# The second layer's output products as seven sums of half the tokens (Strassen), in a kernel whose in-products already go that way

## Chip, cores, metric

One core of a Trainium2 chip. The metric is the device time of one launch in microseconds; below is the median of three runs. All data start and end in device memory.

## What is computed

The reference is a linear-attention block (decayed scores in blocks of 64, a running state) followed by two feed-forward layers in float32. Only the layers matter here; tokens are 1536, of which the first 512 are a block of their own and the other 1024 (two blocks of 512) are "the token pair":

```python
x = x @ w_in                     # 1536 x 512 by 512 x 2048
x = np.maximum(x, 0.0) ** 2
x = x @ w_out                    # layer 1, back to 512
gate = 1.0 / (1.0 + np.exp(-(x @ w_gate)))   # layer 2, 512 x 1536
val = x @ w_val
out = gate * val @ w_out         # 1536 x 1536 by 1536 x 512
```

## The kernel before

Float32 products are made of reduced-precision float32 (`F32R`): each operand is split into a high part (a cast, on ScalarE) and a low part (what the cast lost, a subtraction on VectorE), and three products high x high, high x low, low x high are added up in PSUM. So every 128 x 128 tile of weights costs three matmuls for a block of 512 tokens.

Program order is written out by hand. A list of dated jobs (`at(pos, job)`) hangs on a clock that counts the planned TensorE time (`passed(us)`); a job is put into the engines' queues when the clock passes its date. The date only places the job among its neighbours in each queue: an engine takes its queue strictly in order and runs ahead as far as data and free buffers allow. Loads and stores go through SyncE's queue (SP).

Order of work: attention; layer 1 for the first 512 tokens (`step_1`); layer 1's in-products for the token pair by Strassen (`strassen`, one key is one 256 x 256 product in seven blocks of six matmuls); its output products (`pair_out(1)`); then the same for layer 2: `step_2`, `strassen` with twelve keys (gate and val in turn), `pair_out(2)`. T5 is the planned moment at which the last of these begins.

In a key, block A11 is snapped by ScalarE (`snap`, giving `s1`), then come S1 (`s5`), S2 (`s2`), S4, S3, A12 and A22. VectorE makes the sums (`total`, L559). A gate sum goes through a sigmoid on ScalarE (L651), a val sum is multiplied with the gate on VectorE (L655) and stored to device memory (`g_dram`). Blocks S1 and S4 share a bank, A11, S2, S3 and A22 another: the next block on a bank starts only when its reader is done.

`pair_out(2)` walks the twelve rows f of 128 hidden units. For each, `load_out` fetches the stored product (128 x 1024) and the output weights (128 x 512), `split_out` splits both, and 24 matmuls of 512 columns add to eight banks (four rows of output, two blocks of tokens). With the last f, each bank is copied and sent out as it ends.

Of the kernel before, what the change touches and what calls it, by code (L numbers as in the profile page):

```python
# [34 lines left out]
MM = 0.2267  # L35
# [5 lines left out]
def retention_moe_kernel(  # L41
# [24 lines left out]
    nc = tc.nc  # L66
# [5 lines left out]
    NF2 = w2.shape[0]  # L72
# [5 lines left out]
    wp = ctx.enter_context(tc.tile_pool(name="wp", bufs=27))  # L78
# [16 lines left out]
    def at(pos, fn):  # L95
        agenda.append((pos, len(agenda), fn))
# [7 lines left out]
    def passed(us):  # L104
        clock[0] += us
        flush()
# [140 lines left out]
    xr = {}  # L247
# [190 lines left out]
    def evacuate(ph):  # L438
# [17 lines left out]
    a_t, as_t, s_t = {}, {}, {}  # L456
    g_dram = {
        1: dram.tile([NF1, P, 2, TB], F32, name="g1"),
        2: dram.tile([NF2, P, 2, TB], F32, name="g2"),
    }  # L460
    A11, A12, A22 = (0, 0), (0, 1), (0, 3)
    S3, S4, S1, S2 = (1, 0), (1, 1), (1, 2), (1, 3)
# [155 lines left out]
        held.clear()  # L618

    held = []  # L620

    def keep_g(ph, f, t, g):
        held.append(lambda: nc.sync.dma_start(out=g_dram[ph][f, :, t], in_=g))

    def pair_in_1(i):
        def use(di, t, c, in_psum):
# [51 lines left out]
    def prepare_out(ph, f, pos):  # L678
        at(pos - 16.0, lambda: load_out(ph, f))
        at(pos - 6.5, lambda: split_out(f))  # L680

    def pair_out(ph):
        nf = NF1 if ph == 1 else NF2
        acc = {}
        for f in range(nf):
            (wh, wl), (gh, gl) = wos_t.pop(f), gs_t.pop(f)
            first, last = f == 0, f == nf - 1
            order = [(e, t) for t in range(2) for e in range(4)]
            if last:
                order = [(e, t) for e in range(4) for t in range(2)]  # L690
            for e, t in order:
                if first:
                    acc[e, t] = bank()
                for i, (a, b) in enumerate(((wh, gh), (wh, gl), (wl, gh))):
                    nc.tensor.matmul(  # L695
                        acc[e, t], lhsT=a[:, e * P : (e + 1) * P], rhs=b[:, t, :],
                        start=first and i == 0, stop=last and i == 2,
                    )
                passed(3 * MM)
                if last:  # L700
                    copy = nc.scalar.copy if t == 0 else nc.vector.tensor_copy
                    if ph == 1:
                        copy(xr[t + 1][:, e, :], acc[e, t])
                        continue
                    o = unit("o")
                    dst = out[e, :, (t + 1) * TB : (t + 2) * TB]
                    if (e, t) != (3, 1):
                        copy(o, acc[e, t])
                        (nc.scalar if t == 0 else nc.sync).dma_start(out=dst, in_=o)
                        continue  # L710
                    a, b = slice(0, TB // 2), slice(TB // 2, TB)
                    nc.scalar.copy(o[:, a], acc[e, t][:, a])
                    nc.vector.tensor_copy(o[:, b], acc[e, t][:, b])
                    nc.scalar.dma_start(out=dst[:, a], in_=o[:, a])
                    nc.sync.dma_start(out=dst[:, b], in_=o[:, b])


    order = ORDER
    lead = LEAD
# [18 lines left out]
    for k in range(lead, NCH):  # L738
        a, b = SLOTS[k - lead]
# [196 lines left out]
```

## Time and profile before

| | |
|---|---|
| median of three runs | 603.05 us (602.11 to 603.96) |
| span of the profiled execution, first to last instruction | 599.4 us; no time of its own is listed for it, and 3.65 us lie between it and the median |
| TensorE matmuls busy | 582.6 us, 97% of the span |
| TensorE weight loads busy (beside matmuls) | 478.8 us, 80% |
| VectorE busy | 448.6 us, 75% |
| ScalarE busy | 332.5 us, 55% |
| output products, both layers (L695) | 672 matmuls of 512 columns |

A matmul's recorded length (390 ns) is longer than its distance to the next, since matmuls overlap; the distance from start to start is what counts. An engine's idle time matters only where TensorE waits for it.

### The profile page before, as it was taken

The numbers are of one execution on the slowest core, as the hardware profiler recorded it, in microseconds if no ns is written. First come the engines' busy times: TensorE is split into PE (matmuls) and PEld (weight loads), VectorE is DVE, ScalarE is ACT, GpSimd is POOL, SyncE is SP. The second block draws the span as 40 slices with busy tenths as digits, with TensorE's granted clock in tenths as the row PEclk, the third lists the DMA queues.
The fourth block names the chain that finished last, engine by engine and source line by source line (L and its number), as shares of the span: only waits on it lengthen the run. The fifth ranks groups of instructions, "written<-read, shape, count | busy, mean of one in ns | idle before, by whom it ended". The sixth has DMA issues, their size and how long they took to land.

```text
span 599.4 us, 8496 instructions
## 1 busy us (share of the span) xinstructions
PE 582.6 (97%) x3076; PEld 478.8 (80%) x3076; DVE 448.6 (75%) x673; ACT 332.5 (55%) x525; POOL 36.9 (6%) x34
## 2 busy tenths in 40 slices
PE   7799999999899999999999999999999999999997
PEld 7677878887678888888888888888888888888885
DVE  0699998999888868988877788694778787569101
ACT  0367787988556456756557654554464455537101
POOL 1672212100000000000000000000000000000000
PEclk9899999999999999999999999999999999999999
DMA  7996898682145377999978945511332422658003
GB/s 212 402 418 232 306 309 331 237 297 87 57 121 208 107 240 271 408 414 415 410 276 279 312 170 172 163 50 54 122 106 106 140 81 80 209 187 357 0 1 141
DMA packets 53578, 127.19 MB, mean 212 GB/s; under 512 B 5784, under 2 KB 7584, under 8 KB 53536
## 3 DMA queue, kind: packets, MB, share of 16 engines
q1 hardware_dynamic: 52376, 124.41, 57.9%
q10 hardware_dynamic: 1160, 2.24, 1.1%
q8 instruction: 24, 0.39, 0.3%
q14 instruction: 18, 0.15, 0.1%
HBM read 90.96 MB, written 35.66 MB: 211 GB/s over the span
## 4 chain that ended last, share of the span: by engine, by line
PE 87%; DVE 4%; DMA 2%; POOL 2%; issue 2%; ACT 1%; SPq 0%; ACTq 0%; POOLq 0%; DVEq 0%
PE p L545 30%; PE p L695 25%; PE p L386 17%; PE p L400 12%; DMA kv<-in_kv 1%; POOL kd L278 1%; PE p L329 1%; PE p L322 1%; POOL qd L285 1%; DMA lam_sb<-in_lam 1%; PE p L264 1%; DVE wlo L374 1%; DVE al L526 1%; DVE m L175 1%; ACT ah L520 1%
## 5 line engine op out<-in xcount | busy, mean ns | idle before, releaser
L545 PE MATMUL p<-xcl,ah 128*128 128x512 f32 x280 | 109.1, 390 | 2.5 <-DVE xcl L469 2.5
L545 PE MATMUL p<-xch,ah 128*128 128x512 f32 x280 | 109.4, 391 | 0.4 <-ACT s L554 0.2
L545 PE MATMUL p<-xch,al 128*128 128x512 f32 x280 | 109.0, 389 | 0.0
L695 PE MATMUL p<-g2h,whi 128*128 128x512 f32 x224 | 87.1, 389 | 0.0
L695 PE MATMUL p<-g2l,whi 128*128 128x512 f32 x224 | 87.1, 389 | 0.0
L695 PE MATMUL p<-g2h,wlo 128*128 128x512 f32 x224 | 87.1, 389 | 0.0
L545 PEld LDWEIGHTS p<-xcl,ah 128*128 128x128 f32 x280 | 52.6, 188 | 13.5 <-DVE xcl L469 2.9
L545 PEld LDWEIGHTS p<-xch,ah 128*128 128x128 f32 x280 | 52.5, 188 | 12.9 <-ACT s L554 1.4
L545 PEld LDWEIGHTS p<-xch,al 128*128 128x128 f32 x280 | 52.6, 188 | 11.0
L559 DVE TENSOR_TENSOR c<-p,s 128x512 f32<-128x512 f32 x60 | 41.2, 688 | 25.3 <-PE p L545 21.4
L554 ACT COPY s<-p 128x512 f32<-128x512 f32 x60 | 35.0, 586 | 37.4 <-PE p L545 37.4
L167 DVE CUSTOM_DVE_ANT_0 u<-m,r 128x1024 uint16<-128x1024 uint16 x68 | 49.5, 728 | 2.7
L374 DVE TENSOR_TENSOR wlo<-u,whi 128x512 fp32r<-128x512 f32 x68 | 46.1, 707 | 7.0 <-ACT whi L372 5.7
L150 ACT ACTIVATE j<-raw 128x512 f32<-128x512 f32 x68 | 45.6, 671 | 10.2 <-issue 5.3
L175 DVE SCALAR_TENSOR_TENSOR m<-j,m 128x512 int32<-128x512 int32 x68 | 49.5, 728 | 1.2
L151 ACT ACTIVATE r<-raw 128x512 int32<-128x512 uint32 x68 | 45.2, 665 | 8.7 <-PE p L695 5.5
L695 PEld LDWEIGHTS p<-g2l,whi 128*128 128x128 f32 x224 | 42.0, 188 | 8.8
L695 PEld LDWEIGHTS p<-g2h,whi 128*128 128x128 f32 x224 | 42.0, 188 | 8.7
L695 PEld LDWEIGHTS p<-g2h,wlo 128*128 128x128 f32 x224 | 42.0, 188 | 8.7
L372 ACT CAST whi<-u 128x512 fp32r<-128x512 f32 x68 | 39.0, 616 | 13.7 <-DVE u L167 13.2
L386 PE MATMUL p<-xh,wlo 128*128 128x512 f32 x160 | 43.2, 392 | 1.1 <-DVE wlo L374 1.1
L386 PE MATMUL p<-xh,whi 128*128 128x512 f32 x160 | 43.8, 395 | 0.0
(87 smaller groups left out, 911.6 us busy)
## 6 DMA issues: line engine op xcount, KB each, us to landing
raw<-in_w SPq DMA_DIRECT2D x68, 512.0 KB, 7.1
w<-u SPq DMA_DIRECT2D x68, 256.0 KB, 4.0
u<-w SPq DMA_DIRECT2D x64, 256.0 KB, 5.5
g<-g SPq DMA_DIRECT2D x56, 256.0 KB, 4.4
g<-g SPq DMA_DIRECT2D x28, 512.0 KB, 7.5
a<-w SPq DMA_DIRECT2D x20, 512.0 KB, 4.3
kv<-in_kv SPq DMA_DIRECT2D x12, 512.0 KB, 8.6
qk<-in_qk SPq DMA_DIRECT2D x10, 512.0 KB, 5.7
```

Source lines behind the costliest of these rows:

```text
L150: nc.scalar.activation(j, t[:, :, 1].bitcast(F32), AF.Copy, scale=2.0**-112)
L151: nc.scalar.activation(r, t[:, :, 0].bitcast(mybir.dt.uint32), AF.Copy, scale=2.0**-29)
L167: nc.vector.tensor_tensor(out=w.bitcast(I32), in0=m, in1=r, op=ALU.add)
L175: lambda: nc.vector.scalar_tensor_tensor(out=m, in0=j, scalar=-(2**31), in1=m, op0=ALU.bitwise_and, op1=ALU.bitwise_or),
L372: nc.scalar.copy(hi, src)
L374: lambda lo=lo, src=src, hi=hi: nc.vector.tensor_tensor(out=lo, in0=src, in1=hi, op=ALU.subtract)
L386: nc.tensor.matmul(acc, lhsT=a[:, kk * P : (kk + 1) * P], rhs=b[:, kk, :], start=i == 0, stop=i == 11,)
L400: nc.tensor.matmul(acc[e], lhsT=a[:, e * P : (e + 1) * P], rhs=b, start=first and i == 0, stop=last and i == 2,)
L545: nc.tensor.matmul(acc, lhsT=w[:, col, kk * P : (kk + 1) * P], rhs=x[:, kk, :], start=start and i == 0, stop=stop and i == 5, skip_group_c ...
L554: nc.scalar.copy(s, acc)
L559: nc.vector.tensor_tensor(out=c, in0=acc, in1=s, op=ALU.add)
L695: nc.tensor.matmul(acc[e, t], lhsT=a[:, e * P : (e + 1) * P], rhs=b[:, t, :], start=first and i == 0, stop=last and i == 2,)
```

## The change

Layer 2's output products for the token pair are made by Strassen as well, over pairs i of hidden rows, halves e of the 512 outputs and the two blocks of tokens. `pair_out(2)` is replaced by `blocks_out`. The tokens of each block are cut into two halves h of 256, worked one after the other; for each h seven sums of 128 x 512 (two row tiles p of 256 columns) are kept in seven banks over all six i, and combined after the last i on VectorE into the four output blocks. Each i needs seven combinations of weights (`set_w`, once, kept for both halves) and seven of stored products (`set_g`, once for each h), each split into high and low. Weight sets 0 and 1 are made during the Strassen part before, set 2 at its end, sets 3 to 5 during the first half. Stored products lie in pairs now, so that one load brings the four quarters that a set needs. The pool `wp` has 28 buffers for 27.

```diff
+    HB = TB // 2
+    MH = 0.1152
...
+    def set_w(i, pos, lead):
...
+        def combine():
+            w0, w1 = (w.rearrange("p (e c) -> p e c", e=2) for w in wq_t[i])
+            s = quad(4, "ws", F32)
...
+            tt(out=s[:, 0], in0=w0[:, 1], in1=w0[:, 0], op=ALU.subtract)
+            tt(out=s[:, 2], in0=w0[:, 1], in1=w1[:, 1], op=ALU.add)
+            tt(out=s[:, 3], in0=w1[:, 1], in1=s[:, 0], op=ALU.add)
+            tt(out=s[:, 1], in0=w1[:, 0], in1=s[:, 3], op=ALU.subtract)
...
+            nc.scalar.copy(r[:, 0], w0[:, 0])
+            nc.scalar.copy(r[:, 1:3], w1)
+            nc.scalar.copy(c, s)
...
+            tt(out=rl[:, 0], in0=w0[:, 0], in1=rh[:, 0], op=ALU.subtract)
+            tt(out=rl[:, 1:3], in0=w1, in1=rh[:, 1:3], op=ALU.subtract)
+            tt(out=cl, in0=s, in1=ch, op=ALU.subtract)
+
+        at(pos - lead, load)
+        at(pos - 7.5, combine)
+        at(pos - 5.5, high)
+        at(pos - 3.4, low)
+
+    def set_g(h, i, pos):
...
+            tt(out=t[:, 0:2], in0=g[:, 0:1].to_broadcast([P, 2, HB]), in1=g[:, 1:4:2], op=ALU.subtract)
+            tt(out=t[:, 2], in0=g[:, 3], in1=t[:, 0], op=ALU.subtract)
+            tt(out=t[:, 3], in0=g[:, 2], in1=t[:, 2], op=ALU.subtract)
...
+            nc.scalar.copy(r, g[:, 1:4])
+            nc.scalar.copy(c, t)
...
+            nc.vector.tensor_tensor(out=rl, in0=g[:, 1:4], in1=rh, op=ALU.subtract)
+            nc.vector.tensor_tensor(out=cl, in0=t, in1=ch, op=ALU.subtract)
+
+        at(pos - 14.0, load)
+        at(pos - 7.0, combine)
+        at(pos - 5.4, high)
+        at(pos - 3.2, low)
+
+    def blocks_out():
...
+                for k, ((wp_, wc), (gp_, gc)) in where.items():
+                    if i == 0:
+                        acc[k] = bank()
+                    for p in range(2):
+                        for n, (a, b) in enumerate(((0, 0), (0, 1), (1, 0))):
+                            nc.tensor.matmul(
+                                acc[k][:, p * HB : (p + 1) * HB],
+                                lhsT=ws[a][wp_][:, wc, p * P : (p + 1) * P],
+                                rhs=gs[b][gp_][:, gc],
...
+                        passed(3 * MH)
+                        if last and h == 1 and k == 4:
+                            add("c21", 4, "u3", slice(p * HB, (p + 1) * HB))
+                            put(v["c21"], 1, 0, p)
...
+                    if k == 1:
+                        v["s1"] = unit("s1")
+                        nc.scalar.copy(v["s1"], acc[1])
+                    elif k == 2:
+                        add("c11", 2, "s1")
...
-        for f in range(NF2):
-            prepare_out(2, f, T5 + 24 * MM * f)
+        step = 42 * MH
+        for i in range(NF2 // 2):
+            pos = (T4 + 45.0, T4 + 75.0, T5 - 1.0)[i] if i < 3 else T5 + step * i - 1.5
+            set_w(i, pos, 14.0)
+            for h in range(2):
+                n = h * NF2 // 2 + i
+                set_g(h, i, T5 + step * n - (1.0 if n else 0.0))
...
-        pair_out(2)
+        blocks_out()
```

The sums are worked in the order 1, 2, 6, 5, 7, 3, 4; sums 1, 2 and 3 read the stored products as they are (`gqr`), the others their combinations (`gqt`). In the changed kernel lines behind 618 move by two or more (L655 becomes L657).

Three places show what moves in the queues. First VectorE's queue around the last key of the Strassen part, before: `c<-p,s` are the key's sums, `g<-c,r` the products with the gate, `wlo` and `g2l` low halves for the output part. The second `c<-p,s` is the one that block A22 waits for.

```order
L675 TENSOR_TENSOR wlo<-u,whi 128x512
L676 TENSOR_TENSOR g2l<-g_5222,g2h 128x1024
L559 TENSOR_TENSOR c<-p,s 128x512
L655 TENSOR_TENSOR g<-c,r 128x512
L559 TENSOR_TENSOR c<-p,s 128x512
L655 TENSOR_TENSOR g<-c,r 128x512
L559 TENSOR_TENSOR c<-p,s 128x512
L655 TENSOR_TENSOR g<-c,r 128x512
```

The same place on VectorE now, with the low halves of weight set 2 (`wqs`) and of token set 0 (`gqr`, `gqt`) and the combining of token set 1 (`gt`):

```order
L726 TENSOR_TENSOR wqs<-ws,wqs 128x1024
L559 TENSOR_TENSOR c<-p,s 128x512
L657 TENSOR_TENSOR g<-c,r 128x512
L757 TENSOR_TENSOR gqr<-gq,gqr 128x768
L758 TENSOR_TENSOR gqt<-gt,gqt 128x1024
L743 TENSOR_TENSOR gt<-gq 128x512
L744 TENSOR_TENSOR gt<-gq,gt 128x256
L745 TENSOR_TENSOR gt<-gq,gt 128x256
L559 TENSOR_TENSOR c<-p,s 128x512
L657 TENSOR_TENSOR g<-c,r 128x512
L559 TENSOR_TENSOR c<-p,s 128x512
```

Five operations stand between the first and the second sum where one stood.

Second, ScalarE's queue where a val key follows a gate key in the Strassen part, before: sigmoids `r`, high halves `ah`, copies `s` of the key's banks, of which the last two are `s5` and `s2`.

```order
L651 ACTIVATE r<-c 128x512 x3
L520 CAST ah<-a 128x1024
L554 COPY s<-p 128x512
L651 ACTIVATE r<-p 128x512
L520 CAST ah<-as 128x1024
L554 COPY s<-p 128x512 x2
```

Now, at the key that holds weight set 1 (`wq`, `ws`):

```order
L653 ACTIVATE r<-c 128x512 x3
L520 CAST ah<-a 128x1024
L554 COPY s<-p 128x512
L716 CAST wq<-wq 128x256
L717 CAST wq<-wq 128x512
L718 CAST wq<-ws 128x1024
L653 ACTIVATE r<-p 128x512
L520 CAST ah<-as 128x1024
L554 COPY s<-p 128x512 x2
```

Three casts stand between the first copy and the sigmoid ahead of the last two.

Third, VectorE's queue for one i of the first half, where before there were two operations for each f (`wlo` and `g2l`, as in the first piece); here i = 3, and i = 4 and 5 read alike:

```order
L702 TENSOR_TENSOR ws<-wq 128x256
L703 TENSOR_TENSOR ws<-wq 128x256
L704 TENSOR_TENSOR ws<-wq,ws 128x256
L705 TENSOR_TENSOR ws<-wq,ws 128x256
L743 TENSOR_TENSOR gt<-gq 128x512
L744 TENSOR_TENSOR gt<-gq,gt 128x256
L745 TENSOR_TENSOR gt<-gq,gt 128x256
L724 TENSOR_TENSOR wqr<-wq,wqr 128x256
L725 TENSOR_TENSOR wqr<-wq,wqr 128x512
L726 TENSOR_TENSOR wqs<-ws,wqs 128x1024
L757 TENSOR_TENSOR gqr<-gq,gqr 128x768
L758 TENSOR_TENSOR gqt<-gt,gqt 128x1024
```

Two f make one i, so four operations have become twelve.

## Rows read from the trace of the kernel before

**Rows 1.** The page: span, and TensorE's granted clock in 40 slices.

```profile
span 599.4 us, 8496 instructions
...
PEclk9899999999999999999999999999999999999999
```

**Rows 2.** Stretches: length, then busy time of PE, PEld, DVE, ACT, POOL, clock, DMA.

```profile
505.00:515.00 10.00, 10.00 (x45) 8.27 (x45) 8.53 (x14) 4.13 (x6) 0.00 (x0) 1.00 0.60 156
...
540.00:550.00 10.00, 10.00 (x46) 8.29 (x45) 9.48 (x11) 8.38 (x11) 0.00 (x0) 1.00 1.03 412
...
560.00:570.00 10.00, 10.00 (x46) 8.29 (x45) 0.00 (x0) 0.00 (x0) 0.00 (x0) 1.00 0.00 0
```

**Rows 3.** The chain that ended last: start, length, engine, line, count.

```profile
417.94 111.78 PE p L545 x492
529.72 64.61 PE p L695 x285
```

**Rows 4.** Timeline of TensorE: sixteen 128-column products at two clocks.

```profile
13.43 1.87 PE L264 MATMUL p<-qk 64*128 64x128 f32 x16 [0.23 <-DMA qk<-in_qk]
...
118.31 1.16 PE L264 MATMUL p<-qk 64*128 64x128 f32 x16
```

**Rows 5.** Groups of the page: weight loads of the output products (busy, mean ns, idle).

```profile
L695 PEld LDWEIGHTS p<-g2l,whi 128*128 128x128 f32 x224 | 42.0, 188 | 8.8
```

**Rows 6.** Timeline of VectorE, one key: start, length, operation.

```profile
506.45 0.69 DVE L559 TENSOR_TENSOR c<-p,s 128x512 f32<-128x512 f32 x1 [1.36 <-PE p L545]
507.18 0.69 DVE L655 TENSOR_TENSOR g<-c,r 128x512 f32<-128x512 f32 x1
507.78 0.68 DVE L559 TENSOR_TENSOR c<-p,s 128x512 f32<-128x512 f32 x1
...
511.04 0.42 DVE L513 TENSOR_TENSOR as<-a 128x256 f32<-128x256 f32 x1
511.38 0.41 DVE L514 TENSOR_TENSOR as<-as 128x256 f32<-128x256 f32 x1
...
512.65 1.21 DVE L526 TENSOR_TENSOR al<-a,ah 128x1024 fp32r<-128x1024 f32 x1
513.78 1.21 DVE L526 TENSOR_TENSOR al<-as,ah 128x1024 fp32r<-128x1024 f32 x1
```

**Rows 7.** Timeline of ScalarE in the key before the last two.

```profile
500.31 0.63 ACT L651 ACTIVATE r<-c 128x512 f32<-128x512 f32 x1 [0.73 <-DVE c L559]
500.84 1.03 ACT L520 CAST ah<-a 128x1024 fp32r<-128x1024 f32 x1
501.78 0.58 ACT L554 COPY s<-p 128x512 f32<-128x512 f32 x1
...
503.73 0.59 ACT L554 COPY s<-p 128x512 f32<-128x512 f32 x1
```

**Rows 8.** Timeline, last key: the sum, and block A22's first matmul.

```profile
527.31 0.68 DVE L559 TENSOR_TENSOR c<-p,s 128x512 f32<-128x512 f32 x1
...
528.20 0.39 PE L545 MATMUL p<-xch,ah 128*128 128x512 f32 x1
```

**Rows 9.** Timeline of TensorE: its longest wait in a Strassen part.

```profile
158.32 0.50 PE L545 MATMUL p<-xcl,ah 128*128 128x512 f32 x1 [2.52 <-DVE xcl L469]
```

**Rows 10.** A stretch behind the last product, columns as in rows 2.

```profile
597.00:597.50 0.50, 0.00 (x0) 0.00 (x0) 0.00 (x0) 0.00 (x0) 0.00 (x0) 0.87 0.82 285
```

**Rows 11.** Timeline of the end, all engines.

```profile
592.57 0.39 PE L695 MATMUL p<-g2h,wlo 128*128 128x512 f32 x1
...
593.00 0.59 ACT L708 COPY o<-p 128x512 f32<-128x512 f32 x1 [0.77 <-PE p L695]
...
594.61 0.39 PE L695 MATMUL p<-g2h,wlo 128*128 128x512 f32 x1
...
595.81 0.42 DVE L713 COPY o<-p 128x256 f32<-128x256 f32 x1 [1.44 <-ACT o L712]
596.26 0.33 SPq L715 DMA_DIRECT2D out_t<-o  x1
```

More of the change, by code (lines that the diff above doesn't have):

```diff
@@ L680, in prepare_out, with quad, load, high @@
         at(pos - 6.5, lambda: split_out(f))
+    HB = TB // 2
+    MH = 0.1152
+    wq_t, wqs_t, gq_t, gqs_t = {}, {}, {}, {}
+    def quad(n, name, dt=F32R):
+        return wp.tile([P, n, HB], dt, tag="w", name=name)
+    def set_w(i, pos, lead):
+        def load():
+            w = wq_t[i] = [unit("wq"), unit("wq")]
+            for n in range(2):
+                nc.sync.dma_start(out=w[n], in_=w32[2][2 * i + n, 2])
+        def combine():
+            w0, w1 = (w.rearrange("p (e c) -> p e c", e=2) for w in wq_t[i])
+            s = quad(4, "ws", F32)
+            wq_t[i] = w0, w1, s
+            tt = nc.vector.tensor_tensor
+            tt(out=s[:, 0], in0=w0[:, 1], in1=w0[:, 0], op=ALU.subtract)
+            tt(out=s[:, 2], in0=w0[:, 1], in1=w1[:, 1], op=ALU.add)
+            tt(out=s[:, 3], in0=w1[:, 1], in1=s[:, 0], op=ALU.add)
+            tt(out=s[:, 1], in0=w1[:, 0], in1=s[:, 3], op=ALU.subtract)
+        def high():
+            w0, w1, s = wq_t[i]
+            if i < 2:
+                tags = (("xh", "xl"), ("xr1", "xr2"))[i]
+                both = [xp.tile([P, 8, HB], F32R, tag=t, name="wq") for t in tags]
+                wqs_t[i] = [(t[:, 0:3], t[:, 3:7]) for t in both]
+            else:
+                wqs_t[i] = [(quad(3, "wqr"), quad(4, "wqs")) for _ in range(2)]
+            r, c = wqs_t[i][0]
+            nc.scalar.copy(r[:, 0], w0[:, 0])
+            nc.scalar.copy(r[:, 1:3], w1)
+            nc.scalar.copy(c, s)
+        def low():
+            w0, w1, s = wq_t.pop(i)
+            (rh, ch), (rl, cl) = wqs_t[i]
+            tt = nc.vector.tensor_tensor
+            tt(out=rl[:, 0], in0=w0[:, 0], in1=rh[:, 0], op=ALU.subtract)
[5 more added lines that the diff above has]
+        at(pos - 3.4, low)
@@ new lines, in set_g, with load, combine, high @@
+    def set_g(h, i, pos):
+        def load():
+            g = gq_t[h, i] = quad(4, "gq", F32)
+            nc.sync.dma_start(out=g, in_=g_dram[2][i, :, :, h * HB : (h + 1) * HB])
+        def combine():
+            g = gq_t[h, i]
+            t = quad(4, "gt", F32)
+            gq_t[h, i] = g, t
+            tt = nc.vector.tensor_tensor
+            tt(out=t[:, 0:2], in0=g[:, 0:1].to_broadcast([P, 2, HB]), in1=g[:, 1:4:2], op=ALU.subtract)
+            tt(out=t[:, 2], in0=g[:, 3], in1=t[:, 0], op=ALU.subtract)
+            tt(out=t[:, 3], in0=g[:, 2], in1=t[:, 2], op=ALU.subtract)
+        def high():
+            g, t = gq_t[h, i]
+            gqs_t[h, i] = [(quad(3, "gqr"), quad(4, "gqt")) for _ in range(2)]
+            r, c = gqs_t[h, i][0]
+            nc.scalar.copy(r, g[:, 1:4])
+            nc.scalar.copy(c, t)
+        def low():
+            g, t = gq_t.pop((h, i))
+            (rh, ch), (rl, cl) = gqs_t[h, i]
+            nc.vector.tensor_tensor(out=rl, in0=g[:, 1:4], in1=rh, op=ALU.subtract)
[4 more added lines that the diff above has]
+        at(pos - 3.2, low)
@@ new lines, in blocks_out, with put, add @@
+    def blocks_out():
+        where = {
+            1: ((0, 0), (0, 0)), 2: ((0, 1), (0, 1)), 6: ((1, 3), (1, 2)), 5: ((1, 2), (1, 0)),
+            7: ((1, 0), (1, 1)), 3: ((1, 1), (0, 2)), 4: ((0, 2), (1, 3)),
+        }
+        ni = NF2 // 2
+        for h in range(2):
+            acc = {}
+            v = {}
+            def put(c, r, t, p=None):
+                ee = slice(0, 2) if p is None else slice(p, p + 1)
+                col = (t + 1) * TB + h * HB
+                eng = nc.sync if r == t else nc.scalar
+                eng.dma_start(
+                    out=out[2 * r : 2 * r + 2, :, col : col + HB].rearrange("e p t -> p e t")[:, ee],
+                    in_=c.rearrange("p (e t) -> p e t", e=2)[:, ee],
+                )
+            def add(name, a, b, ee=slice(0, 512)):
+                if name not in v:
+                    v[name] = unit(name)
+                nc.vector.tensor_tensor(
+                    out=v[name][:, ee], in0=acc[a][:, ee], in1=v[b][:, ee], op=ALU.add
+                )
+            for i in range(ni):
+                ws, gs = wqs_t[i], gqs_t.pop((h, i))
+                last = i == ni - 1
+                for k, ((wp_, wc), (gp_, gc)) in where.items():
[7 more added lines that the diff above has]
+                                rhs=gs[b][gp_][:, gc],
+                                start=i == 0 and p == 0 and n == 0,
+                                stop=last and n == 2,
+                                skip_group_check=True,
+                            )
+                        passed(3 * MH)
+                        if last and h == 1 and k == 4:
+                            add("c21", 4, "u3", slice(p * HB, (p + 1) * HB))
+                            put(v["c21"], 1, 0, p)
+                    if not last:
+                        continue
+                    if k == 1:
[3 more added lines that the diff above has]
+                        add("c11", 2, "s1")
+                        put(v["c11"], 0, 0)
+                    elif k == 6:
+                        add("u2", 6, "s1")
+                    elif k == 5:
+                        add("u4", 5, "u2")
+                    elif k == 7:
+                        add("c22", 7, "u4")
+                        put(v["c22"], 1, 1)
+                        add("u3", 7, "u2")
+                    elif k == 3:
+                        add("c12", 3, "u4")
+                        put(v["c12"], 0, 1)
+                    elif h == 0:
+                        add("c21", 4, "u3")
+                        put(v["c21"], 1, 0)
@@ L701, in pair_out @@
                     copy = nc.scalar.copy if t == 0 else nc.vector.tensor_copy
[L702 to L715, printed above, removed]
+                    copy(xr[t + 1][:, e, :], acc[e, t])
     order = ORDER
@@ L866, in retention_moe_kernel @@
             step_2(f)
-        for f in range(NF2):
-            prepare_out(2, f, T5 + 24 * MM * f)
+        step = 42 * MH
+        for i in range(NF2 // 2):
+            pos = (T4 + 45.0, T4 + 75.0, T5 - 1.0)[i] if i < 3 else T5 + step * i - 1.5
+            set_w(i, pos, 14.0)
+            for h in range(2):
+                n = h * NF2 // 2 + i
+                set_g(h, i, T5 + step * n - (1.0 if n else 0.0))
         uses = [use for i in range(NF2 // 2) for use in pair_in_2(i)]
         strassen(keys, uses, (None, lambda: close(2)))
-        pair_out(2)
+        blocks_out()
         flush()
```

8 lines of the change are left out of this document (5 added, 3 removed).

## Prediction

> **What bounds the kernel now.** Read the profile from the top. The span is 599.4 us and TensorE's granted clock is full (2.4 GHz) in nearly every slice [rows 1]. The chain of what ended last then says which engine sets the end: from the second layer's Strassen part on it is TensorE alone, 492 products in 111.78 us and then 285 of the 288 output products in 64.61 us, 226.7 ns each [rows 3]. Nothing waits there, so fewer columns through TensorE are worth their full time, and any wait put before a product costs its full time. Third, the stretches: in the Strassen part VectorE is busy 8.53 of 10 us; in the output part it does all its splitting in the first 20 us (9.48 of 10 us), and 30 us later has nothing to do [rows 2]. The change gives VectorE more to do in both, so the question is whether it keeps up. TensorE's own number cannot answer that.
>
> The times below start at T5, where the output part begins (529.56 us). A "key" is one of the twelve Strassen products of gate and val, seven blocks of six matmuls, 9.52 us.
>
> **Removed and added on TensorE.** 288 products of 512 columns go: 288 x 226.7 ns = 65.3 us [rows 3]. 504 of 256 columns come. No row has a 256-column product. At 2.4 GHz its columns take 106.7 ns. A 512-column one takes 213.3 ns for its columns and 13.4 ns more; if those 13.4 ns come once per product, 256 columns take 120.1 ns, if they shrink with the columns 113.4. I take 115: 58.0 us, **-7.3 us**; the ends are 53.8 and 60.5 us. Above them stands the weight load, recorded at 188 ns [rows 5]. That is no spacing: sixteen 128-column products with sixteen 128-column loads pass in 1.16 us [rows 4], in two halves of the array that alternate, so about 0.11 to 0.14 us each in a half. But these loads fill 64 rows and mine 128, so 188 stays as a rival.
>
> The Trainium skill ("Perfetto Trace Analysis", Identifying the Most-Contended Engine) judges TensorE's headroom by the busy share of its weight loads. Here they fill 8.29 of 10 us [rows 2], and the change loads 504 times for 288; by that rule the part would be bound by loads and last 504 x 188 ns = 94.8 us. The sixteen loads above speak against it, without settling it.
>
> **Prices on VectorE and ScalarE.** Operations of one queue overlap a little, so I price them from start to start. VectorE: 512 columns 0.60 us, 0.73 where the next reads the result; 256 columns 0.34 (then 0.45); 1024 columns 1.13 [rows 6]. 768 columns lie between: 0.87. ScalarE: 512 columns 0.52, 1024 columns 0.95 [rows 7]; between and below, 0.73 for 768 and 0.27 for 256.
>
> A weight set (`set_w`, six of them) is on VectorE 3 x 0.34 + 0.45 = 1.47 to combine and 0.34 + 0.60 + 1.13 = 2.07 for the low halves, 3.54 together; ScalarE's high halves take 0.27 + 0.52 + 0.95 = 1.74. A token set (`set_g`, twelve) is 0.73 + 0.45 + 0.34 = 1.52 and 0.87 + 1.13 = 2.00, 3.52 together; ScalarE 1.68. One step of TensorE (seven sums x 6) lasts 42 x 0.115 = 4.83 us. In the first half's steps for i = 3, 4, 5 VectorE must do a weight set and a token set, **7.06 us of work in 4.83**. The queue is in order, so what is late stays late.
>
> **Where TensorE will wait.** Five places.
>
> 1. Weight sets 0 and 1 stand inside the Strassen part. In the last key of that kind, before, ScalarE goes from the sigmoid at 500.31 through two splits and a copy to the copy at 503.73, which ends 504.32, with no gap [rows 7]; the block S4, which overwrites that bank, starts four blocks before the key's end, two keys ahead of T5: 529.56 - 19.04 - 4 x 1.36 = 505.08. So 0.76 us is spare. Set 1 puts 1.47 us of combining before the sum that the sigmoid reads, and 1.74 us of high halves between the copies: 3.2 - 0.76 = 2.4, of which small gaps between the sigmoids take part; I put 2.0. Set 0 lies in a key without sigmoids; it delays the same copy by less, 0.9. **+2.9.**
>
> 2. The last key. The block A22 overwrites the bank that `total(x, s5)` reads, so it waits for that sum. Before, the sum starts at 527.31, ends 527.99, and A22 starts at 528.20 [rows 8]. Now weight set 2's low halves, token set 0's low halves and token set 1's combining stand ahead of it. From the end of block S1 (T5 - 6.8): product to reader 0.2 (593.00 less 592.57 and a 0.227 product [rows 11]), copy and high halves to 2.55 (S2's copy behind them makes S4 wait 0.4), the last low half to 3.8, a sum and a product to 5.15, set 0's low halves to 7.15, set 1's combining to 8.7, the sum to 9.3. A22 was due at 5.44 + 0.4: **+0.4 and +3.4**.
>
> 3. The output part, from its start: VectorE still has the last product of the Strassen part (to 1.2), set 1's low halves (3.2, due 4.8), set 2 (7.05 with 0.3 for ScalarE's high half), then pairs of 7.06: their first low half is there at 13.0, 20.1 and 27.1. TensorE wants them at 14.6, 19.4 and, with the wait before, 25.0: 0, 0.7 and 2.1, **+2.8**. Behind these lies the rest of the first half, which only shifts; token sets 6 to 11 need 3.52 of 4.83 and VectorE recovers.
>
> 4. From half 0 to half 1. Seven sums on VectorE (five of them with a dependent follower, 4.8 us) come on top of token set 7 in one step: 8.3 in 4.83. Half 1's banks come free only as these go: with what is spare I put **+1.9** in three waits.
>
> 5. The end. The sum `c21` is read by halves, but both halves lie in one bank, so TensorE's last three products wait for the add of the first half, which stands behind four other sums: **+1.5**. After the last product there is then one 256-column add (0.42) and one issue on ScalarE's queue. Before, from the start of the last product at 594.61 to the last issue at 596.26 was 1.65 us, with two copies in turn [rows 11]; now about 0.33 + 0.42 + 0.05 = 0.8, and the product is 0.1 shorter: **-0.75**.
>
> Loads cost nothing: a set's 512 KB is issued 14 us ahead, of which the wait in the queue leaves enough; a gather that lands late would delay VectorE in the first half by its lateness, since nothing covers it there.
>
> **Sum.** -7.3 + 2.9 + 3.8 + 2.8 + 1.9 + 1.5 - 0.75 = +4.85. The span would be 604.2 us; the median of the runs is 603.05, 3.65 above the profiled span, so **607.9 us**.
>
> **Rivals.**
>
> *The waits are covered (faster).* VectorE's queue is not tied to TensorE's place, and runs ahead where data lie ready: in the output part before, its splitting was over when half the products were still to come [rows 2]. If it enters the part at least 7 us ahead, places 1 to 4 vanish: 603.05 - 7.3 + 1.5 - 0.75 = 596.5. It decides where VectorE's work between T5 - 5 and T5 + 25 fits into 30 us. Against it: the last low half of weight set 2 (1.1), seven sums and products (4.6), token sets 0 to 2 from the low halves of 0 on (9.0) and three pairs (21.2) are 36 us by the prices above. Chance 0.07.
>
> *The waits before T5 are smaller.* If the sums find room that the rows don't show, places 1 and 2 shrink to 2.3 us in all: 603.5, within 0.3% of before, which is about what a measurement of this kernel can tell from no change. Chance 0.15.
>
> *The clock falls.* After the last product the clock went to its lower level within 2.5 us of idleness [rows 10], yet the wait of 2.52 us at 158.32 [rows 9] left its slice at full clock [rows 1]. A22's wait of 3.4 us is longer than both. At the lower level sixteen products took 1.87 us for 1.16 [rows 4]. For A22 alone that is about 1 us, which delays VectorE's last product and with it the whole queue; the steps after it have 2.8 us of waiting to give. About +1.2: 609.1. The Trainium skill ("TensorE: Matmul & The Clock Gate", Why this matters for your kernels) has the rule that gaps between bursts of matmuls bring the half clock back; here the wait of 2.52 us did not, the idleness after the end did. Chance 0.1.
>
> *Weight loads bind.* 504 x 188 ns = 94.8 us for 58.0, with VectorE's waits hidden behind it: about 603.05 + 29.5 = 632. Against it [rows 4]. Chance 0.03.
>
> **How the numbers follow.** The main case has 0.65. Its own spread is from the product's price (106.7 to 120.1 ns; half of the 504 products lie where VectorE sets the pace, so -2 to +1.5) and from ten restarts of TensorE at 0.1 us: 605 to 611. To hold 8 in 10 the range takes in the smaller waits and the clock: 603.7 to 610.8. Faster by over 0.3% 0.07; within 0.3% 0.15; slower 0.78.
>
> **What would show it.** TensorE's products L800 at about 115 ns from start to start where nothing waits; a gap of some 3 us before the last block A22, ended by VectorE's `c` L559; waits before the first sums of steps 4 and 5 ended by `gqr` L757; short waits ended by L788 after half 0; VectorE without idle time from T5 - 4 to T5 + 28. Wrong: L800 spaced by 188 ns, or VectorE idle in that stretch.

## The result, and the profile after

The changed kernel takes 610.12 us in the median of four runs (608.42 to 611.16), the kernel before 602.58 in four: ratio 1.013, 95% interval 1.0104 to 1.0156. It is 7.5 us slower where 4.85 was forecast; the time lies in the range (603.7 to 610.8) near its upper end.

The page of the profiled execution (610.41 us), against [rows 1]:

```profile
span 608.3 us, 9029 instructions
...
PEclk9699999999999999999999999999999999989999
```

The chain that ended last (start, length, engine, line, count), against [rows 3]:

```profile
420.15 29.93 PE p L545 x132
460.36 22.09 PE p L545 x96
491.06 37.03 PE p L545 x162
539.25 16.33 PE p L800 x126
578.02 21.76 PE p L800 x179
```

Where the chain before had one piece of 492 products and one of 285, it is cut at 460, 491, 539 and 578 us: at each cut TensorE waited. The part before the first row has the same work in both kernels, yet it ends 2.2 us later here (420.15 for 417.94). That is scatter and not the change: over the ten runs below, which share this part, it ends between 417.3 and 422.3 us; the three latest of the eleven, this one among them, show 6 in the second slice of `PEclk`, in which the clock comes back from its lower level, the others 7 or 8. So I compare **from the start of the Strassen part to the end of the span**: 599.4 - 417.94 = 181.5 us before, 608.3 - 420.15 = 188.2 now, **+6.7 us**. Each of these is one profiled execution, but the measure repeats where kernels share their work: block A22 starts 117.1 us behind the start of the Strassen part in this kernel (537.30 - 420.15) and in three of those below (e4, e6 and e11).

What TensorE waited for from there on (in total, times, longest):

```profile
PE p L545 <- DVE c L559: 3.2, 1, 3.2
PE p L545 <- ACT s L554: 2.9, 3, 1.8
PE p L800 <- DVE c L788: 1.4, 1, 1.4
PE p L800 <- DVE u L788: 1.0, 2, 0.5
PE p L800 <- DVE gqr L757: 0.4, 2, 0.2
```

Before, this view of the same stretch is empty. A wait costs 0.27 us more than its idle time: idle time begins where the record of the product ahead ends, which is 0.16 us behind the moment the next one could start (0.39 less 0.227), and the first product after a wait takes 0.34 us to the next (460.36 to 460.70), 0.11 too many.

The longest of them, VectorE and TensorE at the last block A22, against [rows 8]:

```profile
533.04 0.95 DVE L757 TENSOR_TENSOR gqr<-gq,gqr 128x768 fp32r<-128x768 f32 x1
...
533.91 1.22 DVE L758 TENSOR_TENSOR gqt<-gt,gqt 128x1024 fp32r<-128x1024 f32 x1
535.04 0.68 DVE L743 TENSOR_TENSOR gt<-gq 128x512 f32<-128x512 f32 x1
...
536.56 0.68 DVE L559 TENSOR_TENSOR c<-p,s 128x512 f32<-128x512 f32 x1
...
537.30 0.50 PE L545 MATMUL p<-xch,ah 128*128 128x512 f32 x1 [3.19 <-DVE c L559]
```

It is the picture of the forecast: low halves of token set 0 and combining of set 1 ahead of the sum, and A22 behind it. (The section on the change counts five operations between the two sums; six stand there, the product with the gate and five more.)

Stretches of the output part (PE, PEld, DVE, ACT, POOL, clock), against [rows 2]:

```profile
540.00:550.00 10.00, 10.00 (x78) 10.00 (x78) 9.57 (x17) 4.52 (x7) 0.00 (x0) 0.91 0.77 262
550.00:560.00 10.00, 10.00 (x86) 10.00 (x85) 9.90 (x16) 4.47 (x8) 0.00 (x0) 1.00 0.18 54
560.00:570.00 10.00, 9.80 (x82) 9.59 (x81) 9.50 (x17) 4.88 (x6) 0.00 (x0) 1.00 0.33 107
570.00:580.00 10.00, 8.82 (x69) 8.21 (x68) 9.69 (x15) 2.94 (x4) 0.00 (x0) 1.00 0.40 120
```

VectorE is busy 9.5 to 9.9 of 10 us for 40 us in a row, ScalarE 2.9 to 4.9, and the clock is below full behind A22's wait.

### The profile page after: what moved, and what is told of

It is laid out like the page before. It is cut to its first block, busy times and chain, and to the rows that moved or that the text cites. A ratio compares the mean times of both kernels' runs of the same rounds, so it can differ in the third digit from the quotient of the medians.

```text
span 608.3 us, 9029 instructions
## 1 busy us (share of the span) xinstructions
PE 582.6 (96%) x3292; PEld 487.7 (80%) x3292; DVE 496.7 (82%) x762; ACT 344.4 (57%) x540; POOL 35.5 (6%) x34
## 4 chain that ended last, share of the span: by engine, by line
PE 80%; DVE 11%; ACT 3%; DMA 3%; issue 2%; SPq 0%; POOL 0%; DVEq 0%; ACTq 0%; POOLq 0%
PE p L545 26%; PE p L386 18%; PE p L848 14%; PE p L400 12%; PE p L800 6%; PE p L322 1%; DMA raw<-in_w 1%; PE p L329 1%; PE p L264 1%; DVE c L559 1%; ACT ah L520 1%; DVE c L788 1%; DMA lam_sb<-in_lam 1%; DVE u L788 1%; ACT s L554 1%
## 5 line engine op out<-in xcount | busy, mean ns | idle before, releaser
L848 PE MATMUL p<-g2h,whi 128*128 128x512 f32 x128 | 49.8, 389 | 0.0
L848 PE MATMUL p<-g2l,whi 128*128 128x512 f32 x128 | 49.8, 389 | 0.0
L848 PE MATMUL p<-g2h,wlo 128*128 128x512 f32 x128 | 49.8, 389 | 0.0
L386 PE MATMUL p<-xl,whi 128*128 128x512 f32 x160 | 42.8, 389 | 0.0
L386 PEld LDWEIGHTS p<-xh,wlo 128*128 128x128 f32 x160 | 29.9, 188 | 8.1 <-DVE wlo L374 1.8
L386 PEld LDWEIGHTS p<-xl,whi 128*128 128x128 f32 x160 | 30.0, 188 | 6.3
```

The costliest lines, as they stand in the source:

```text
L386: nc.tensor.matmul(acc, lhsT=a[:, kk * P : (kk + 1) * P], rhs=b[:, kk, :], start=i == 0, stop=i == 11,)
L848: nc.tensor.matmul(acc[e, t], lhsT=a[:, e * P : (e + 1) * P], rhs=b[:, t, :], start=first and i == 0, stop=last and i == 2,)
```

## Experiments

All numbers "from the Strassen part" are the span less the start of that part in the run's own trace, from one profiled execution each, with 181.5 for the kernel before and 188.2 for the changed one. Medians have the early scatter in them as well; ratios are to runs of the kernel before from the same session.

| run | what | median us | ratio to before, 95% | from the Strassen part |
|---|---|---|---|---|
| e2 | before, 256-column products | 606.81 | 1.0075 (1.0049 to 1.0101) | 605.8 - 420.55 = 185.3 |
| e3 | the sum first | 610.34 | 1.0133 (1.0101 to 1.0165) | 606.0 - 417.64 = 188.4 |
| e4 | sets 3 to 5 left out | 605.63 | 1.0066 (1.0041 to 1.0091) | 602.9 - 417.33 = 185.6 |
| e5 | both | 602.04 | 0.9995 (0.9978 to 1.0011) | 599.3 - 417.86 = 181.4 |
| e6 | own bank at the end | 610.24 | 1.0111 (1.0085 to 1.0137) | 606.4 - 418.51 = 187.9 |
| e7 | other dates for sets 0 and 1 | 608.65 | 1.0096 (1.0072 to 1.0119) | 606.3 - 420.06 = 186.2 |
| e8 | sets on GpSimd | 615.33 | 1.0214 (1.0190 to 1.0238) | 612.5 - 419.05 = 193.5 |
| e9 | sets made early | 598.32 | 0.9939 (0.9921 to 0.9957) | 595.5 - 417.85 = 177.7 |
| e10 | e9, last two pairs together | 597.68 | 0.9923 (0.9905 to 0.9941) | 595.6 - 419.10 = 176.5 |
| e11 | e4 with the wait filled | 604.87 | 1.0061 (1.0040 to 1.0082) | 606.8 - 422.29 = 184.5 |

### The price of a 256-column product

```diff
 def pair_out(ph):                                    # kernel before
+                for c in halves:                     # ph == 2: two of 256 columns
                     for i, (a, b) in enumerate(((wh, gh), (wh, gl), (wl, gh))):
                         nc.tensor.matmul(
-                            acc[e, t], lhsT=a[:, e * P : (e + 1) * P], rhs=b[:, t, :],
+                            acc[e, t][:, c], lhsT=a[:, e * P : (e + 1) * P], rhs=b[:, t, c],
```

> The kernel before, with each of the 288 output products of 512 columns cut into two of 256 columns (576 products, 576 weight loads), nothing else changed. It prices a 256-column product by itself. Theory (the 13.4 ns beyond the columns come once per product): 576 products at 119.5 to 120 ns in place of 288 at 226.7, 68.8 to 69.1 us in place of 65.3, so 3.6 us slower than before, ratio 1.006. Rival (those 13.4 ns shrink with the columns, and the wider spacing in the changed kernel came from something in it): 115 ns, 66.2 us, 1 us slower, ratio 1.002. Rival (a weight load of 128 rows binds at its recorded 188 ns): 108 us, 43 us slower.

The chain and a stretch of its output part:

```profile
532.39 68.41 PE p L697 x570
```

```profile
560.00:570.00 10.00, 10.00 (x85) 10.00 (x85) 0.00 (x0) 0.00 (x0) 0.00 (x0) 1.00 0.00 0
```

68.41 / 570 = 120.0 ns, and the whole is 3.8 us longer. So the 13.4 ns come once per product, and a product of half the columns is dearer than half a product. The weight loads' column reads 10.00 of 10 and yet nothing is spaced by 188 ns. The Trainium skill ("Perfetto Trace Analysis", Identifying the Most-Contended Engine) names this column as a measure of TensorE's headroom. As it was read in the prediction (a part full of loads lasts as long as their records add up to), the rule does not hold here: the loads fill 100% by the record, and the products come every 120 ns.

### Is a wait a price of its own, or does VectorE's work set the end?

Four kernels answer this: the changed one, one with the order in VectorE's queue mended, one with work taken out of the queue, and both.

```diff
 def set_g(h, i, pos):                                # e3, e5
-        at(pos - 7.0, combine)
-        at(pos - 5.4, high)
-        at(pos - 3.2, low)
+        at(T5 - 2.5 if n == 1 else pos - 7.0, combine)
+        at(T5 - 2.4 if n == 1 else pos - 5.4, high)
+        at(T5 - 2.6 if n == 0 else pos - 3.2, low)
...
-            set_w(i, pos, 14.0)                      # e4, e5
+            if i < 3:
+                set_w(i, pos, 14.0)
...
-                ws, gs = wqs_t[i], gqs_t.pop((h, i))
+                ws, gs = wqs_t[min(i, 2)], gqs_t.pop((h, i))
```

> The changed kernel with dates moved so that token set 0's low halves and all work on token set 1 stand behind the sum that block A22 waits for; the same instructions otherwise. Theory (from the last key to the middle of the output part VectorE's total work sets the end, and a wait only shows where TensorE meets it): the 3.35 us wait before A22 goes, the clock stays full, TensorE reaches the output part 4 to 5 us earlier, and waits for low halves again at steps 1 to 5 (about 0.5, 0, 0.8, 2.0 and 2.0 us); the half switch stays where it was in time; the whole is 610.1 as the changed kernel, within 0.8 us. Rival (each wait is a price of its own, so that what goes at A22 is gained): 3.4 us for the wait and 1.4 us for the half clock behind it, 605.3 us.

Waits of e3 from the Strassen part on:

```profile
PE p L801 <- DVE gqr L757: 3.0, 5, 1.8
PE p L545 <- ACT s L554: 2.9, 3, 1.8
PE p L801 <- DVE c L789: 1.4, 1, 1.4
PE p L801 <- DVE u L789: 1.0, 2, 0.5
```

A22's wait of 3.2 us is gone and the clock stays full there, TensorE starts the output part 3.7 us earlier after the start of the Strassen part (532.79 - 417.64 = 115.2 for 539.05 - 420.15 = 118.9), and **nothing is gained**: 188.4 us for 188.2. The time is back as waits for the low halves `gqr`, four of them ahead of the half switch. (The expectation had the clock full throughout; it fell later instead, behind the wait of 1.78 us, as the last section shows.) The place where both kernels meet is the first product of step 5, in e3 and in the changed kernel:

```profile
556.27 2.61 PE L801 MATMUL p<-gqr,wqr 128*128 128x256 f32 x11 [1.78 <-DVE gqr L757]
...
563.34 0.86 PE L801 MATMUL p<-gqr,wqr 128*128 128x256 f32 x5 [0.28 <-DVE gqr L757]
```

```profile
565.97 0.50 PE L800 MATMUL p<-gqr,wqr 128*128 128x256 f32 x2 [0.20 <-DVE gqr L757]
```

563.34 - 417.64 = 145.7 us and 565.97 - 420.15 = 145.8 us behind the start of the Strassen part: the same moment, whatever TensorE did before it. VectorE, with the same work in another order, is there at the same time.

> The changed kernel with weight sets 3, 4 and 5 left out (loads, combining, high and low halves); set 2 is used in their place, so the output is not the reference's. It takes 10.6 us of work from VectorE in the first half, dates unchanged. Theory: the waits of step 5 (0.5 us) and of the half switch (2.0 us) go, the A22 wait (3.35) and the half clock behind it stay: 2.5 us less than the changed kernel, 607.6 us. Rival (the half switch waits for the seven banks as such, not for VectorE's backlog): only 0.5 us less, 609.6.

> The moved dates of the second run and the left-out weight sets 3 to 5 of the third together; the output is not the reference's. Theory (VectorE's work and the order of it are one cost): now the A22 wait, the half clock and the waits behind are all gone, about 7.5 us less than the changed kernel where the moved dates alone gave nothing and the left-out sets alone 2.5: 602.6 us, with one wait of some 0.5 us at step 1 left. Rival (each wait a price of its own): the sum of the two gains that the single runs show, whatever these are.

The waits of e4, then of e5:

```profile
PE p L545 <- DVE c L559: 3.2, 1, 3.2
PE p L545 <- ACT s L554: 2.9, 3, 1.8
PE p L800 <- DVE c L788: 1.4, 1, 1.4
```

```profile
PE p L545 <- ACT s L554: 2.9, 3, 1.8
PE p L801 <- DVE c L789: 1.7, 1, 1.7
PE p L801 <- DVE gqr L757: 0.2, 1, 0.2
```

With less work alone, step 5 and the half switch wait no longer (2.6 us less, 2.5 expected; the medians differ by 4.5, with the early scatter in them); A22's wait stays. So the half switch waited for VectorE's backlog, not for banks as such. The left-out sets spare ScalarE's casts and some loads too, which no run took away by themselves; but ScalarE was less than half busy in these stretches of the changed kernel, and e9 below moves more bytes and has none of these waits. With both, 6.7 us go (7.5 expected), where the single edits gave -0.2 and 2.6. The theory that prices each wait by itself would have the sum, 2.4.

### Places 1 and 5

```diff
 def set_w(i, pos, lead):                             # e7
+        s, late = (6.0, 2.8) if i < 2 else (0.0, 0.0)
         at(pos - lead, load)
-        at(pos - 7.5, combine)
-        at(pos - 5.5, high)
-        at(pos - 3.4, low)
+        at(pos - 7.5 + s, combine)
+        at(pos - 5.5 + s + late, high)
+        at(pos - 3.4 + s + late, low)
 def blocks_out():                                    # e6
+                        if h == 1 and k == 4:
+                            acc[0] = bank()
...
+                        own = h == 1 and k == 4 and p == 1
...
-                                acc[k][:, p * HB : (p + 1) * HB],
+                                acc[0 if own else k][:, p * HB : (p + 1) * HB],
```

> The changed kernel with weight sets 0 and 1 dated otherwise inside the Strassen part: loads at the old dates, combining 6.0 us later, high and low halves 8.8 us later. The same instructions. Theory (place 1 lies ahead of the stretch that VectorE bounds, and moves that stretch with it, so what goes there is gained): the waits of 0.93 and 1.99 us shrink to one of about 0.5, the A22 wait and all behind it stay as long as they are: 2.4 us less than the changed kernel, 607.7 us. Rival (VectorE's total work decides here too): under 0.5 us less, 610.

1.9 us less from the Strassen part, where 2.4 was expected and under 0.5 by the rival. The waits for the copies shrink from 2.9 us in three to 0.5 in two; the waits for `gqr` grow from 0.4 to 0.8. What lies ahead of VectorE's full stretch moves that stretch with it, and most of it is gained.

> The changed kernel, in which the second half of the last sum (c21, last half of the tokens) has a bank of its own, so that the last three products need not wait for the add of the first half. Nothing else. Theory (VectorE's queue ends the kernel: c22, u3, c12 and the two adds of c21 stand one behind the other): the wait of 1.55 us before the last three products goes, but the last issue comes some 1.5 us behind the last product where it was 0.7, so 0.7 us less than the changed kernel from the start of the Strassen part, which the medians can hardly show. Rival (the wait is the whole price): 1.6 us less.

0.3 us less from the Strassen part, under both the 0.7 expected and the rival's 1.6. The last three products no longer wait, but the end of e6, and below it the last issues of the changed kernel, read:

```profile
600.82 0.76 PE L803 MATMUL p<-gqt,wqr 128*128 128x256 f32 x5
...
601.53 1.34 DVE L788 TENSOR_TENSOR c<-p,u 128x512 f32<-128x512 f32 x3
602.25 1.63 ACTq L780 DMA_DIRECT2D out_t<-c  x3
```

```profile
604.03 1.82 ACTq L780 DMA_DIRECT2D out_t<-c  x3
```

The last product starts at 601.30 (600.82 + 0.76 less a record of 0.28), and VectorE's last three adds run to 602.87, behind it. Behind the adds come the three stores that ScalarE's queue issues one after the other: they are out 185.4 us behind the start of the Strassen part (602.25 + 1.63 - 418.51), in the changed kernel 185.7 (604.03 + 1.82 - 420.15). So VectorE's adds and the issues behind them are the end, whether TensorE waits for one of the adds or not.

### Where to put VectorE's work

> A version meant to be better than both: the combining of all six weight sets and the low halves of sets 0 to 4 go from VectorE to GpSimd, which does nothing here; sets are dated earlier to leave GpSimd time (its operations of 512 columns took 1.2 to 1.6 us, of 256 columns 0.96, in the kernel before); the moved dates of the second run; token set 3 loaded ahead of the last stores; the own bank of the last sum. Theory (VectorE's work from the last key to the half switch was the price): no wait over 0.6 us is left before the end, 9 us less than the changed kernel, 2.4 us less than before: 600.2 us, ratio 0.996. Rival (VectorE and GpSimd slow each other on their reads): VectorE's 0.69 us for 512 columns and 1.22 for 1024 grow while GpSimd works, by a third 6 us more in the 25 us from the output part's start, and the waits at steps 3 to 5 are back: 605 us or more. Rival (GpSimd itself is late): waits ended by GpSimd's low halves of sets 3 and 4.

```diff
 def set_w(i, pos, lead):                             # e8; not shown: its dates, set 3's load, e3's order, e6's bank
-            tt = nc.vector.tensor_tensor
+            tt = (nc.gpsimd if i in (0, 1, 2, 3, 4, 5) else nc.vector).tensor_tensor
...
-            tt = nc.vector.tensor_tensor
+            tt = (nc.gpsimd if i in (0, 1, 2, 3, 4) else nc.vector).tensor_tensor
```

The first rival came true, and worse: 5.3 us slower than the changed kernel from the Strassen part. Groups of VectorE's operations from 525 to 600 us (busy, mean ns of one), first of the changed kernel, then of e8:

```profile
L758 DVE TENSOR_TENSOR gqt<-gt,gqt 128x1024 fp32r<-128x1024 f32 x12 | 14.7, 1222 | 1.8 <-ACT gqt L752 1.8
...
L743 DVE TENSOR_TENSOR gt<-gq 128x512 f32<-128x512 f32 x12 | 8.2, 684 | 0.0
...
L657 DVE TENSOR_TENSOR g<-c,r 128x512 f32<-128x512 f32 x3 | 2.1, 692 | 0.1
```

```profile
L760 DVE TENSOR_TENSOR gqt<-gt,gqt 128x1024 fp32r<-128x1024 f32 x12 | 17.2, 1435 | 1.8 <-ACT gqt L754 1.8
...
L745 DVE TENSOR_TENSOR gt<-gq 128x512 f32<-128x512 f32 x11 | 10.8, 981 | 0.0
...
L657 DVE TENSOR_TENSOR g<-c,r 128x512 f32<-128x512 f32 x3 | 4.2, 1384 | 0.1
L559 DVE TENSOR_TENSOR c<-p,s 128x512 f32<-128x512 f32 x3 | 2.1, 684 | 4.7 <-ACT s L554 4.7
```

`gt` takes 981 ns for 684, the product `g` 1384 for 692; single ones go to 2.88 us, while one that fell where GpSimd had nothing to do (538.02 us) took 0.68. The sums `c<-p,s`, which read one operand from PSUM, take the same 684 ns as ever, also the two of them that ran beside GpSimd (530.19 and 533.12 us). The Trainium skill ("GPSIMD Engine Reference", Specifications) says that GpSimd shares its SBUF interfaces with VectorE and that the two contend when VectorE reads two SBUF inputs. These rows agree. Waits of TensorE ended by GpSimd itself, the second rival, did not come. Other ways to share the work between the two were not tried.

The next runs put the work where VectorE itself has time. In the Strassen part it had 1.5 us or more free in 10 [rows 2].

```diff
 def set_w(i, pos, lead):                             # e9, e10; not shown: dates, e3's order, e6's bank
+            if i > 2:
+                for n in range(2):
+                    nc.sync.dma_start(out=set_dram[i - 3, n], in_=kept[i][n][:, 0:7].bitcast(F32))
...
+        def back():
+            wqs_t[i] = [(quad(3, "wqr"), quad(4, "wqs")) for _ in range(2)]
+            for n in range(2):
+                r, c = wqs_t[i][n]
+                nc.sync.dma_start(out=r.bitcast(F32), in_=set_dram[i - 3, n, :, 0:3])
+                nc.sync.dma_start(out=c.bitcast(F32), in_=set_dram[i - 3, n, :, 3:7])
...
+            steps = [[n] for n in range(ni)]         # e10 alone
+            if h == 1:
+                steps[-2:] = [[ni - 2, ni - 1]]
```

> A version meant to be better than both, with VectorE's work taken to where VectorE has room and not to GpSimd: weight sets 3, 4 and 5 are made in the Strassen part too, one in every second key like sets 0 and 1, stored to device memory and loaded back in the first half (1.8 MB each); their high halves are cast in two portions 4.3 us apart, so that no more than 0.8 us stands before a copy of a key's bank; the moved dates of the second run; the own bank of the last sum. Same results as the changed kernel. Theory (VectorE's total work between the last key and the half switch was the price, and in the Strassen part there are 1.5 us of VectorE free in 10): from the start of the Strassen part 3.6 us less than before and 10 less than the changed kernel, 599.1 us, ratio 0.994; waits of 0.4, 0.1 and 0.3 us around the start of the output part, none behind, and an end in which VectorE's queue costs 1.5 us behind the last product. Rival (five more pieces of work in the Strassen part bring waits of 1 to 2 us each, as sets 0 and 1 did): 602 to 606 us. Rival (5.5 MB more of loads delay the token sets in the first half): waits there of 1 us or more, VectorE waiting for gq.

> The kernel of the run before with one thing more: in the second half of the tokens the last two pairs of hidden rows are worked together, sum by sum, so that the seven sums end 1.4 us apart where they ended 0.7 us apart, and VectorE's adds (0.6 us each) keep up. Token set 11 is prepared 5 us earlier for it. Theory: 0.8 us less than the run before, since only one 256-column add stands behind the last product: 598.3 us, ratio 0.993. Rival (token set 11 is late, or the adds were not what the end waited for): no difference or slower.

Both came as expected: 598.32 us (599.1 expected) and 597.68 (598.3), **0.6% and 0.8% faster than before**. Waits and the end of the chain of e10:

```profile
PE p L545 <- ACT s L554: 0.2, 1, 0.2
PE p L830 <- DVE gqr L776: 0.2, 1, 0.2
```

```profile
536.64 55.70 PE p L830 x461
592.36 0.42 DVE c L810
```

461 of the 504 products run in one piece, and a single 256-column add stands behind them. From the Strassen part e10 takes 5.0 us less than the kernel before, of the 6.0 that the products and the shorter end are worth (table below). From e9 to e10 the profiled runs gain 1.2 us (0.8 expected); the medians' difference is inside their scatter. The loads of 5.5 MB brought no wait.

### What A22's wait did to the clock

```diff
 def second(use=use, x=x, key=key):                   # e11: e4 and this
+                if key == (2, NF2 // 2 - 1, 1):
+                    fill = bank()
+                    for n in range(14):
+                        nc.tensor.matmul(
+                            fill, lhsT=s_t[(*key, 0)][0][:, 0, 0:P], rhs=xc["T4"][0][:, 0, :],
+                            start=n == 0, stop=n == 13,
+                        )
                 block(x, key, A22, "T4", False, True)
```

> The run with weight sets 3 to 5 left out (its output is not the reference's), and in the wait before the last block A22 fourteen products of 512 columns to a bank that nobody reads, 3.2 us at full clock, so that TensorE stays at work while it waits for the sum. In that run the granted clock fell to its lower level behind the wait of 3.3 us. Theory (the wait itself brought the clock down, and the first products of the output part then took twice as long): the clock stays full from 530 us on, the output part's first products are 120 ns apart at once, and the time from the start of the Strassen part is 1.4 us less than without the filling, 204 to 205 us less said in medians: 604.2 for 605.6 us. Rival (the clock falls at this place for another reason, such as the change to products of 256 columns): it falls again, and the time is the same within 0.3 us.

(The "204 to 205 us less" in it is a slip of the pen; the 1.4 us ahead of it are meant.) Stretches of e4, where A22 starts at 534.46, and of e11, where it starts at 539.42:

```profile
534.00:536.00 2.00, 1.54 (x7) 1.26 (x8) 1.93 (x4) 1.62 (x2) 0.00 (x0) 0.98 0.01 5
536.00:538.00 2.00, 2.00 (x11) 2.00 (x10) 2.00 (x4) 0.00 (x0) 0.00 (x0) 0.50 0.68 263
538.00:540.00 2.00, 2.00 (x14) 2.00 (x14) 1.97 (x3) 0.00 (x0) 0.00 (x0) 0.67 0.86 255
```

```profile
540.00:542.00 2.00, 2.00 (x15) 1.82 (x14) 1.97 (x5) 0.58 (x1) 0.00 (x0) 1.00 0.34 131
542.00:544.00 2.00, 2.00 (x19) 2.00 (x18) 2.00 (x4) 0.00 (x0) 0.00 (x0) 1.00 0.85 271
```

Filled, the clock stays at its upper level, although the products of 256 columns follow as in e4: the rival is out, and at this place it was the wait. From the start of A22 to the start of the last three products it is 602.91 - 539.42 = 63.5 us for 599.10 - 534.46 = 64.6; those three wait 0.35 us longer for VectorE, so the clock alone is 1.5. The whole is 1.1 us shorter (1.4 expected).

## Why the prediction was nearly right, and where it was wrong

The terms, forecast and measured (waits as idle time plus 0.27 each):

| step of the prediction | forecast | measured |
|---|---|---|
| 504 products for 288 | -7.3 | -4.8 (504 x 120.0 = 60.5 for 65.3) |
| place 1, weight sets 0 and 1 | +2.9 | +3.1 (idle 0.77 and 1.83) |
| place 2, S2's copy and A22 | +0.4 and +3.4 | +0.5 and +3.5 |
| place 3, steps 4 and 5 | +2.8 | +0.5 (one wait, at step 5) |
| place 4, half switch | +1.9 | +2.0 |
| place 5, end | +1.5 | +1.7 |
| tail | -0.75 | -1.2 (4.8 us from the last product to the span's end, now 3.6) |
| clock behind A22 | a rival, about +1.2 in all | +1.4 (16.33 / 126 = 129.6 ns for 120.0 in the chain, 1.2, and the first products; 1.5 by e11) |
| sum | +4.85 | +6.7 |

**Right.** The places, what ends each wait, and VectorE with next to no idle time from the last key into the second half. Places 1, 2, 4 and 5 came within 0.3 us of their prices.

**The product's price** is the step that failed in size: "I take 115". The row had the upper end, 120.1 ns, and e2 shows 120.0. The 13.4 ns come per product, so cutting a product in two adds one such share. This term alone was 2.5 us short, more than the 1.9 by which the whole sum fell short; the clock added 1.4, and place 3 gave 2.3 back. That the time stayed in the range rests on this give and take, which the range had foreseen only in part ("-2 to +1.5" for the product's price), so it is partly luck.

**Place 3 and the clock** belong together. I made the clock a rival of 0.1 because 2.52 us of waiting at 158.32 had left it full; A22's wait of 3.2 us brought it down, and e11 shows that the wait did it. The Trainium skill ("TensorE: Matmul & The Clock Gate", Why this matters for your kernels) has a rule that gaps between bursts of matmuls bring the lower clock back. At A22 the trace agrees; the waits in the last section do not all fit. Yet by the table the clock cost the changed kernel little: TensorE, 1.4 us later and on dearer products, met VectorE's low halves later, and place 3 fell from 2.8 to 0.5. (The changed kernel with this wait filled was not run.) The prediction had said this for the clock ("the steps after it have 2.8 us of waiting to give"), but not for A22's own wait. By e3 the same holds there: remove the wait and steps 1 to 5 take it back. The rival "the waits before T5 are smaller" shows the step that was missing: it takes 4.4 us off the sum for smaller waits at places 1 and 2 and lets place 3 stay as it is. **Places 2 and 3 are one price, set by VectorE's work** between the last key and step 5, and the place where it shows is a matter of order. The stretch begins where ScalarE's casts of weight set 2 are done: VectorE stood idle 1.38 us for them, to 529.10 us. Moving only these casts was not tried.

**A reading that was off:** in the kernel before, VectorE's splitting in the output part lasts 28 us (its last operation ends at 557.5 us) and not 20. The argument there, that half the products were still to come, holds with 28 too.

**Not in the sum:** of the 7.5 us between the medians, 6.7 are found from the Strassen part on; the rest lies within the scatter of the early part, which made 2.2 us between the two profiled executions. I had put the profiled execution of before 3.65 us under the median; in the profiled executions of the eleven later runs, whose own time is listed, about 2.1 us lie outside the span (610.41 and 608.3 for the changed kernel), so that execution was an early one by about 1.5 us.

**The rival "waits are covered"** was built in e9 and e10, with the work moved to where it has cover. The forecast for it, 596.5, is 1.2 us under e10; the dearer products alone are 2.5.

## What to carry to other kernels

When an engine off the path is full over a stretch, add up its work to the point where the path next needs it, and take that as the price: single waits in the stretch can be moved about and give nothing back. Less work on it and a better order pay more together than apart (2.6 and -0.2 us alone, 6.7 together), so an edit that shows no gain by itself isn't refuted. A wait ahead of the stretch is a price of its own (e7). Move such work to where its own engine is idle; giving most of the weight sets' work to the idle GpSimd made VectorE slower.

## What the runs showed of the hardware

- The length of a wait did not decide by itself whether the clock fell. Idle times of 3.19 us (A22) and of 1.78 us (e3, between 256-column products) brought it to its lower level; 1.83 us at 491.06 in the changed kernel and 2.52 us at 158.32 [rows 9] did not (granted clock 1.00 in every stretch from 489 to 497 and from 154 to 166 us). In e3, behind its wait of 1.78 us:

```profile
556.00:558.00 2.00, 1.73 (x8) 1.73 (x9) 2.00 (x5) 0.00 (x0) 0.00 (x0) 0.61 0.71 238
558.00:560.00 2.00, 2.00 (x12) 2.00 (x11) 1.90 (x6) 0.81 (x1) 0.00 (x0) 0.54 0.01 4
```

  What else it depends on was not tried and stays open.
- VectorE's operations with two SBUF operands took up to four times as long beside GpSimd's (2.88 us for 0.68 in e8), sums with a PSUM operand the same time (0.69 and 0.68).
- Weight loads recorded as busy 10.00 of 10 us, 192 ns each in e2's output part, did not bound products that came every 120 ns.
